# Packed attention and a split-precision MLP on one core: two sweeps over halves of w2's rows, with the attention placed between the products

## The chip, the core and the metric

The kernel runs on one core of a Trainium2 chip. Its time is the device time of one execution in microseconds (us). The runs of the kernel before were 879.05, 876.56 and 876.97 us, median 876.97. The engines are TensorE (PE, with its weight loads as PEld), VectorE (DVE), ScalarE (ACT), GpSimd (POOL) and SyncE (SP), whose queue issues every transfer of this kernel.

## The reference

For 8 batches and 8 heads, 32 packed queries `p` attend over the 576 tokens of `k` and `v`, then the 576 tokens of `q` attend over the 32 packed results. The output, laid out as 576 x 512 per batch, is mixed over the tokens with rank 32, and goes through a two-layer MLP with a residual.

```
p_packed = softmax(p k^T / 8) v          # (8, 8, 32, 64)
x        = softmax(q p_packed^T / 8) p_packed   # as (8, 576, 512)
u        = x + (x^T U V)^T
out      = u + relu(u w1) w2             # w1 512 x 2048, w2 2048 x 512
```

`U`, `V`, `w1` and `w2` arrive in 64-bit floating point and are turned into float32 on the chip.

## The kernel before, in words

**The algebra.** The second attention's weights times the packed values are never multiplied out. Per batch the kernel keeps A', the attention weights (8 heads x 32 packed tokens = 256 rows, as two groups `g` of 128 partitions, by 576 tokens) with the token mixing added. u is A' times a block matrix of the packed values, so u w1 is A' times W' (256 x 2048), where W' is the packed values times w1, one *fold* per pair of heads. The MLP of one batch is then, for each of 16 blocks `kt` of 128 hidden columns, `gemm1(kt)` (A' with a piece of W' into PSUM `h_ps`, ReLU) and, one step later, `gemm2(kt-1)` (the ReLU's result with 128 rows of w2, summed over all kt in four PSUM tiles `o` of 128 tokens each). The last 64 tokens of two batches share one further product, `joint`, every second batch. `add_u` adds u itself (`residual`).

**The precision.** Every operand of these products is split into a high and a low part in fp32r, and `mm3` (L74) makes three products: high-high, high-low and low-high (lines 76 to 78 of the profile). ScalarE copies the high part, VectorE or GpSimd subtracts to get the low one. The first attention's score and value products take plain float32 operands (L325, L361, L362).

**The stages.** Stage A goes over 16 units, half a batch each: `k` is turned by VectorE's 32 x 32 transposes (`transposed`, L101), the scores of four heads come from one product with a block-diagonal `bdp` (L325), then come softmax, PE transposes (`a_turn`), the product with `v` (`a_pack`), and the folds of batches 0 to 3 (`fold`, through PSUM and `conv`/`fold` tiles to DRAM, `wsr`). Between them `some_w1` converts w1 (`float32_of`, L67 to L71: one ScalarE and four VectorE operations per 128 x 512 block, and a `split`, L122 to L124). The first batch's second attention (`attention(0)`) runs there too. The tile framework orders stage A; after `manual_schedule` (L534) everything stays in the order in which the code is written.

**The loop.** Over 8 batches of 16 kt each: `gemm1`, `gemm2`, loads and splits of W' pieces (`load_wt`, `split_wt`, L455 and L456), w2's conversion during batch 0, one of 16 steps of the attention of the next batch (`steps`), and the folds of batches 4 to 7 (`later`, with w1 loaded and converted a second time, stored in `wsc`). In the attention `q` is turned by VectorE, split, and multiplied in three fp32r products by a block-diagonal of the packed values (`scores`, L186). `store` copies the sums out through ScalarE and VectorE.

Of the kernel before, what the change touches and what calls it, by code (L numbers as in the profile page):

```python
# [15 lines left out]
DRAM = bass.MemoryType.DRAM  # L16


@with_exitstack
def packed_attention_mixer_kernel(  # L20
# [22 lines left out]

    nc = tc.nc
# [5 lines left out]
    P = 128  # L50
    NB = S // 32
    SM = 512
    NK = DF // P
    NU = 2 * B
    QW = 256
    scale = 1.0 / float(D) ** 0.5
    HALF = ((0, 256), (256, 320))
# [4 lines left out]

    def float32_of(x, t, raw):


        low, high = raw[:, :, 0], raw[:, :, 1]
        nc.scalar.activation(t, high.bitcast(F32), AF.Abs)  # L67
        nc.vector.tensor_single_scalar(t, t, LEAST, op=ALU.max)  # L68
        nc.vector.tensor_scalar(x, t.bitcast(I32), 3, 0x3FFFFFF8, op0=ALU.logical_shift_left, op1=ALU.bitwise_and)  # L69
        nc.vector.scalar_tensor_tensor(x, high, -0x40000000, x, op0=ALU.bitwise_and, op1=ALU.bitwise_or)  # L70
        nc.vector.scalar_tensor_tensor(x, low, 29, x, op0=ALU.logical_shift_right, op1=ALU.bitwise_or)  # L71
        return x.bitcast(F32)
# [10 lines left out]
    psT = ctx.enter_context(tc.tile_pool(name="psT", bufs=2, space=PSUM))  # L83

# [3 lines left out]
    bdq = const.tile([P, 4, P], F32, name="bdq")  # L88
    nc.gpsimd.memset(bdq, 0.0)

    wsr = [dram.tile([2 * H * NP, DF], F32, name=f"wsr{r}", tag=f"wsr{r}") for r in range(2)]
    wsc = {b: dram.tile([H * NP, DF], F32, name=f"wsc{b}", tag=f"wsc{b}") for b in range(B // 2, B)}


    def load_nat(pool, bufs, src, b, g):
        nat = pool.tile([P, NB * D], F32, name="nat", bufs=bufs)
        nc.sync.dma_start(out=nat, in_=src[b, 4 * g:4 * g + 4].rearrange("h (i c) d -> (h i) (c d)", c=NB))
        return nat

    def transposed(t, nat):  # L100
        nc.vector.transpose(  # L101
            t.rearrange("p h (i c) -> p c h i", c=NB),
            nat.rearrange("p (c h l) -> p c h l", h=2, l=32),
        )
        return t


    def weight_tiles(name):
        return [
            tuple(pipe.tile([P, DF], F32R, name=f"{name}{x}{i}", tag=f"w{x}{i}") for x in "hl") for i in range(4)  # L110
        ]

    def conv_tile(dtype):
        return pipe.tile([P, DM], dtype, name="os", bufs=3)

# [672 lines left out]
```

## Time and profile before

| | us |
|---|---|
| median of the three timed runs | 876.97 |
| profiled execution, its own time | 877.77 |
| its span, first to last instruction | 876.0 |
| PE busy | 827.1 (94%) |
| DVE busy | 518.6 (59%) |
| ACT busy | 374.6 (43%) |
| POOL busy | 258.6 (30%) |
| DMA queue, bytes and share of 16 engines | 97.75 MB, 35.9% |

The profiled execution took 0.8 us more than the median of the runs, and 1.8 us of it lie outside the span. Matmuls are pipelined: the next starts before the one ahead has ended, so the profile's mean of one matmul is its length and not what it adds to the engine's time. What it adds is read from the distance of two starts in the timeline. A float32 product leaves two matmul records, an fp32r product one.

### The profile page before, as it was taken

Reading aid. Unit: us, or ns where it says so; the run is one execution under the profiler, and the core shown is the slowest. Engines: PE = TensorE matmul, PEld = TensorE weight load, DVE = VectorE, ACT = ScalarE, POOL = GpSimd, SP = SyncE. Lnnn points to the kernel's source line nnn. Section 1 sums busy time; section 2 is a strip of 40 time slices with the busy share of each in tenths; the row PEclk is TensorE's granted clock in tenths of the full one; section 3 lists DMA queues with packets and bytes.
Section 4 is the critical chain, followed back from the end, with each engine's and each line's share of the span. In section 5 each row is a group of like instructions: output and inputs, shape, how many; then the busy total and the mean of one; then the engine's idle time right before and its main releaser. Section 6 shows DMA issues by size and latency. Waiting matters only on the chain.

```text
span 876.0 us, 12670 instructions
## 1 busy us (share of the span) xinstructions
PE 827.1 (94%) x4480; PEld 708.5 (81%) x4480; DVE 518.6 (59%) x1042; ACT 374.6 (43%) x960; POOL 258.6 (30%) x230
## 2 busy tenths in 40 slices
PE   4779898889999999999999999999999999999997
PEld 2556576677879888888888888988888889889886
DVE  7999986789767875577675443443543524432220
ACT  2557676534444554456554332233332322333220
POOL 3302353545443213132323232323241313221110
PEclk9989999999999999999999999999999999999999
DMA  9769775823333444344453103010301120002001
GB/s 316 237 208 331 213 225 207 256 87 126 128 100 108 120 148 124 97 121 121 124 172 85 52 19 112 26 56 13 112 25 64 62 62 25 25 13 96 25 1 60
DMA packets 59998, 98.55 MB, mean 112 GB/s; under 512 B 12192, under 2 KB 36768, under 8 KB 59936
## 3 DMA queue, kind: packets, MB, share of 16 engines
q1 hardware_dynamic: 59936, 97.75, 35.9%
q8 instruction: 35, 0.57, 0.3%
q14 instruction: 27, 0.22, 0.1%
HBM read 71.52 MB, written 26.21 MB: 112 GB/s over the span
## 4 chain that ended last, share of the span: by engine, by line
PE 72%; DVE 18%; DMA 4%; issue 3%; ACT 3%; SPq 0%; DVEq 0%; ACTq 0%
PE o L78 15%; PE o L76 14%; PE o L77 14%; PE h_ps L76 7%; PE h_ps L77 7%; PE h_ps L78 7%; DVE kT L101 4%; DVE os L70 2%; DVE os L69 2%; DVE os L71 2%; PE w_ps L595 2%; DVE natT L101 2%; DVE os L68 2%; DMA bits<-in_moe_w_ch_dram 1%; PE t_ps L228 1%
## 5 line engine op out<-in xcount | busy, mean ns | idle before, releaser
L643 DVE SCALAR_TENSOR_TENSOR hl<-h_ps,hh 128x256 fp32r<-128x256 f32 x256 | 104.1, 418 | 180.2 <-ACT hh L641 145.0
L78 PE MATMUL o<-w2h,hl 128*128 128x512 f32 x512 | 201.8, 394 | 0.0
L76 PE MATMUL o<-w2h,hh 128*128 128x512 f32 x512 | 200.9, 392 | 0.0
L77 PE MATMUL o<-w2l,hh 128*128 128x512 f32 x512 | 200.4, 391 | 0.0
L641 ACT ACTIVATE hh<-h_ps 128x256 fp32r<-128x256 f32 x256 | 96.1, 383 | 235.0 <-PE h_ps L78 232.0
L76 PE MATMUL h_ps<-ah,fold 128*128 128x256 f32 x496 | 149.7, 302 | 7.5 <-DVE hl L643 7.1
L456 POOL TENSOR_TENSOR fold<-fold 128x512 fp32r<-128x512 f32 x62 | 81.4, 1313 | 230.7 <-ACT fold L455 225.3
L77 PE MATMUL h_ps<-al,fold 128*128 128x256 f32 x496 | 146.5, 295 | 0.0
L78 PE MATMUL h_ps<-ah,fold 128*128 128x256 f32 x496 | 146.0, 294 | 0.0
L78 PEld LDWEIGHTS o<-w2h,hl 128*128 128x128 f32 x512 | 96.1, 188 | 21.3
L77 PEld LDWEIGHTS o<-w2l,hh 128*128 128x128 f32 x512 | 96.4, 188 | 17.6
L76 PEld LDWEIGHTS o<-w2h,hh 128*128 128x128 f32 x512 | 96.3, 188 | 16.7
L76 PEld LDWEIGHTS h_ps<-ah,fold 128*128 128x128 f32 x496 | 93.7, 189 | 14.7 <-DVE hl L643 11.5
L77 PEld LDWEIGHTS h_ps<-al,fold 128*128 128x128 f32 x496 | 93.9, 189 | 2.1
L78 PEld LDWEIGHTS h_ps<-ah,fold 128*128 128x128 f32 x496 | 93.8, 189 | 0.0
L184 POOL TENSOR_TENSOR nlo<-natT,nhi 128x576 fp32r<-128x576 f32 x32 | 46.0, 1453 | 114.8 <-ACT nhi L183 114.8
L68 DVE TENSOR_SCALAR os<-os 128x512 f32<-128x512 f32 (+2 forms) x51 | 39.5, 775 | 35.4 <-ACT os L67 35.4
L325 PE MATMUL s_ps<-kT,bdp 128*128 128x288 f32 x128 | 39.7, 460 | 9.5 <-DVE bdp L316 9.3
L183 ACT CAST nhi<-natT 128x576 fp32r<-128x576 f32 x32 | 20.7, 675 | 56.3 <-DVE natT L101 53.2
L101 DVE STREAM_TRANSPOSE kT<-nat 128x1152 f32<-128x1152 f32 x16 | 37.3, 2330 | 5.8 <-DMA nat<-in_k_dram 5.7
L325 PEld LDWEIGHTS s_ps<-kT,bdp 128*128 128x128 f32 x128 | 26.4, 215 | 17.6 <-issue 9.3
L124 POOL TENSOR_TENSOR w1l<-os,w1h 128x512 fp32r<-128x512 f32 x16 | 21.2, 1328 | 62.3 <-ACT w1h L123 62.3
(145 smaller groups left out, 1419.7 us busy)
## 6 DMA issues: line engine op xcount, KB each, us to landing
bits<-in_moe_w_ch_dram SPq DMA_DIRECT2D x48, 512.0 KB, 4.3
nat<-in_k_dram SPq DMA_DIRECT2D x16, 576.0 KB, 4.9
nat<-in_q_dram SPq DMA_DIRECT2D x16, 576.0 KB, 4.5
vt<-in_v_dram SPq DMA_DIRECT2D x16, 512.0 KB, 5.5
wsr<-fold SPq DMA_DIRECT2D x32, 256.0 KB, 3.7
out_dram<-bits SPq DMA_DIRECT2D x16, 512.0 KB, 3.0
wsc<-bits SPq DMA_DIRECT2D x64, 128.0 KB, 2.2
fold<-wsc SPq DMA_DIRECT2D x32, 256.0 KB, 2.8
```

Source lines behind the costliest of these rows:

```text
L68: nc.vector.tensor_single_scalar(t, t, LEAST, op=ALU.max)
L76: nc.tensor.matmul(ps, lhsT=lh, rhs=rh, start=start, stop=False)
L77: nc.tensor.matmul(ps, lhsT=lh, rhs=rl, start=False, stop=False)
L78: nc.tensor.matmul(ps, lhsT=ll, rhs=rh, start=False, stop=stop)
L101: nc.vector.transpose(t.rearrange("p h (i c) -> p c h i", c=NB), nat.rearrange("p (c h l) -> p c h l", h=2, l=32),)
L124: nc.gpsimd.tensor_tensor(lo, x, hi.bitcast(F32), op=ALU.subtract)
L183: nc.scalar.copy(hi[:, dh], t)
L184: nc.gpsimd.tensor_tensor(lo[:, dh], t, hi[:, dh].bitcast(F32), op=ALU.subtract)
L325: nc.tensor.matmul(s_ps[:, hf, :288], lhsT=bdp[b % 2][:, 2 * g + dh], rhs=kT[:, dh, 288 * hf:288 * hf + 288], start=dh == 0, stop=dh == 1)
L456: nc.gpsimd.tensor_tensor(lo, raw, hi.bitcast(F32), op=ALU.subtract)
L641: nc.scalar.activation(hi, src, AF.Relu)
L643: nc.vector.scalar_tensor_tensor(lo, src, 0.0, hi.bitcast(F32), op0=ALU.max, op1=ALU.subtract)
```

## The change

**Two sweeps.** The loop goes over all 8 batches twice, `sw` 0 with rows 0 to 1023 of w2 (8 kt, `NKS`) and `sw` 1 with the others. Sweep 0 stores the sums of each batch in DRAM (`sums`, `sumj`), sweep 1 loads them (`load_sums`) and adds them on VectorE as it stores the output. A' goes to DRAM after each attention (`asp`) and is loaded again for sweep 1 (`reload_a`). w2's second half is converted during sweep 0, stored split (`w2d`) and loaded between the sweeps (`reload_w2`). w1 is converted once, half of its columns ahead of or at the start of sweep 0, half later; all folds are done by `fold`, four times four per batch pair `r`.

**What runs ahead of the loop.** Only the first attention of batches 0 and 1 (`packs`), the second attention of batch 0, five conversions and four folds. Everything else, `packs` of batches 2 to 7, `attention` of 1 to 7, 27 conversions and 60 folds, stands between the loop's products. The class `Chains` decides where, as the program is built: each chain is a generator that yields an assumed PE cost, a wait and a due time; `side.place(dt)` after every half `gemm1` and every quarter `gemm2` lets the ready chain with the earliest due time take one step; `side.until(name)` places steps until a chain is done, with no product between.

**The attention.** `k` and `q` are turned by PE transposes in pairs of tokens (`turn`, L302) and copied from PSUM by ScalarE and VectorE. The scores take eight float32 products per group, one for each head `h` and parity `r` of the token, 64 rows of `xT` by 32 columns (`scores`, L321), each in a place of its own of the PE array. The product with `v` takes 20 float32 products of 32 columns and 64 values each (L393). Block-diagonals and the split of `q` are gone.

```diff
+    def until(self, name):
+        while not (name in self.done and self.done[name] <= self.now or name in self.flags):
+            if not self.place():
+                self.now += 0.25
...
+    def turn(x, t):
+        pairs = x.rearrange("p a x -> p (a x)")
+        for h2 in range(2):
+            t_ps = bank()
+            for a in range(4):
+                c = 4 * h2 + a
+                nc.tensor.transpose(t_ps[:, P * a:P * a + P], pairs[:, P * c:P * c + P], ident)
+            nc.scalar.copy(t[:, 2 * h2:2 * h2 + 2, HT:HS], t_ps.rearrange("p (h x) -> p h x", h=2))
+            yield 0.45, 0.0
...
+    def scores(lT, t, g):
+        ss = [bank() for _ in range(2)]
+        for h in range(4):
+            hs = slice(32 * h, 32 * h + 32)
+            for r in range(2):
+                rs = slice(64 * r, 64 * r + 64)
+                nc.tensor.matmul(ss[r][hs, :HS], lhsT=lT[rs, g, hs], rhs=t[rs, h, HT * (1 - r):HT * (1 - r) + HS], start=True, stop=True)
+        return ss
...
+            for kk in range(5):
+                rows = P if kk < 4 else 64
+                for h in range(4):
+                    hs = slice(32 * h, 32 * h + 32)
+                    rhs = vk[:, kk, h] if kk < 4 else vx[:rows, 4, D * h:D * h + D]
+                    nc.tensor.matmul(p_ps[hs, :D], lhsT=eT[:rows, kk, hs], rhs=rhs, start=kk == 0, stop=kk == 4)
...
+        for c in cs:
+            for pr in range(4):
+                w_ps = bank()
+                mm3(w_ps, (lwh[:, pr], lwl[:, pr]), w1_slices(pr, c), True, True)
+                st = out_tile()
+                nc.scalar.copy(st, w_ps)
+                nc.sync.dma_start(out=wsr[r, c][P * pr:P * pr + P], in_=st)
+                yield 0.7, 0.0
...
+    together(packs(0))
+    uv = load_uv()
+    together(packs(1))
+    prepare_uv(*uv)
...
+    together(attention(0), in_turn(convert(first, converted), fold(0, (0,))))
...
+                if (sw, b) == (0, 0) and j == 2:
+                    side.until("w1_3_1")
+                    side.until("fold0_1")
...
+                if sw == 0 and b % 2 == 1 and j == 4 and b + 1 < B:
+                    side.until(f"fold{(b + 1) // 2}")
```

Three places of the instruction order show it. The first is PE at the first attention of a unit of stage A, before. `s_ps` are the scores, `kT` the turned keys, `bdp` the block-diagonal queries, `e` the exponentials and `pp_ps` the packed values.

```order
L325 MATMUL s_ps<-kT,bdp_97 128x288 x4
L345 MATMUL t_ps<-ident,e_146 128x128 x4
L346 MATMUL t_ps<-ident,e_146 64x128
L325 MATMUL s_ps<-kT,bdp_97 128x288 x4
L361 MATMUL pp_ps<-vt,eT 128x256 x4
L362 MATMUL pp_ps<-vt,eT 128x256
```

The same engine at a unit of the changed kernel, ahead of its loop (`xt` is a loaded tile, `xT` the turned one, `t_ps` every PSUM tile):

```order
L309 MATMUL t_ps<-ident,xt 128x128 x8
L315 MATMUL t_ps<-ident,xt 128x32 x4
L328 MATMUL t_ps<-xT,pT 32x288 x8
L338 MATMUL t_ps<-ident,e_241 128x128 x4
L340 MATMUL t_ps<-ident,e_241 64x128
L393 MATMUL t_ps<-xt,eT 32x64 x20
L399 MATMUL t_ps<-ident,two 128x128
```

Four products of 128 columns became eight of 32 columns, five of 128 became twenty of 32, and twelve transposes stand ahead. In the order before, the next unit's scores stand ahead of this unit's product with `v`; now one unit stands whole behind the other.

The second place is PE in batch 0 of the changed loop, from the last quarter of `gemm2(0)` to `gemm1(2)`; `w1h` and `w1l` are the split columns 512 to 1023 of w1.

```order
L121 MATMUL o<-w2h_754,hl 128x512
L353 MATMUL t_ps<-ident,pn 128x128 x2
L309 MATMUL t_ps<-ident,xt 128x128 x8
L315 MATMUL t_ps<-ident,xt 128x32 x4
L309 MATMUL t_ps<-ident,xt 128x128 x8
L315 MATMUL t_ps<-ident,xt 128x32 x4
L328 MATMUL t_ps<-xT,pT 32x288 x8
L328 MATMUL t_ps<-xT,ppT 32x288 x8
```

Before, six products of the next batch's scores are all that stands between `gemm2(0)` and `gemm1(2)`:

```order
L78 MATMUL o<-w2h_1446,hl 128x512
L76 MATMUL s_ps<-nhi,bqh 128x288
L77 MATMUL s_ps<-nlo,bqh 128x288
L78 MATMUL s_ps<-nhi,bql 128x288
L76 MATMUL s_ps<-nhi,bqh 128x288
L77 MATMUL s_ps<-nlo,bqh 128x288
L78 MATMUL s_ps<-nhi,bql 128x288
L76 MATMUL h_ps_1650<-ah,wt_1461 128x256
```

The rows of the changed order go on with a third unit of scores, the product with `v` and the twelve products of `fold0_1`, and only then comes `gemm1(2)`.

The third place is DVE, behind the evacuation of `gemm1(1)` in the changed loop (`hjl` is the low part for the joint product; L178 to L184 are the four conversion operations):

```order
L591 SCALAR_TENSOR_TENSOR hjl<-h_ps_924,hjh 128x32
L178 TENSOR_SCALAR ts<-ts 128x512
L179 TENSOR_SCALAR wd<-ts 128x512
L183 SCALAR_TENSOR_TENSOR wd<-bits,wd 128x512
L184 SCALAR_TENSOR_TENSOR wd<-bits,wd 128x512
L178 TENSOR_SCALAR ts<-ts 128x512
L179 TENSOR_SCALAR wd<-ts 128x512
L183 SCALAR_TENSOR_TENSOR wd<-bits,wd 128x512
L184 SCALAR_TENSOR_TENSOR wd<-bits,wd 128x512
L317 COPY xT<-t_ps 64x4x32
```

Before, the same place behind `gemm1(1)` read:

```order
L643 SCALAR_TENSOR_TENSOR hjl<-h_ps_1591,hjh 128x64
L68 TENSOR_SCALAR os<-os 128x512
L69 TENSOR_SCALAR os<-os 128x512
L70 SCALAR_TENSOR_TENSOR os<-bits,os 128x512
L71 SCALAR_TENSOR_TENSOR os<-bits,os 128x512
L196 STREAM_TRANSPOSE e<-s_ps 128x288
```

So one conversion stood between the evacuations of two kt; now seven conversions stand between those of `gemm1(1)` and `gemm1(2)`, with the attention's operations among them.

1015 lines of the change are left out of this document (481 added, 534 removed).

## The prediction

> **What bounds the kernel now.** I read the page first: the busy shares, then the slices.
>
> ```profile
> span 876.0 us, 12670 instructions
> PE 827.1 (94%) x4480; PEld 708.5 (81%) x4480; DVE 518.6 (59%) x1042; ACT 374.6 (43%) x960; POOL 258.6 (30%) x230
> ...
> PE   4779898889999999999999999999999999999997
> ...
> DVE  7999986789767875577675443443543524432220
> ```
>
> PE is full from about the ninth slice; VectorE is nearly full in the first seven. Busy times by stretch give the border (the first column is the stretch, then us, PE, PEld, DVE, ACT, POOL, clock, DMA share, GB/s):
>
> ```profile
> 0.00:50.00 50.00, 29.89 (x116) 21.04 (x116) 43.27 (x76) 22.26 (x57) 15.58 (x26) 0.97 0.86 277
> 100.00:150.00 50.00, 43.03 (x189) 31.54 (x188) 40.84 (x73) 35.43 (x83) 21.83 (x17) 0.94 0.69 219
> 300.00:400.00 100.00, 99.79 (x561) 87.37 (x560) 65.95 (x129) 49.55 (x117) 25.29 (x21) 1.00 0.41 121
> ```
>
> In stage A VectorE and the transfers are near their limit and PE waits; from 300 us PE has no gap. The timeline of PE tells where the loop begins, what one step costs, and where it ends.
>
> ```profile
> 160.18 0.39 PE L78 MATMUL w_ps<-w1h,lwl 128*128 128x512 f32 x1
> 160.41 0.28 PE L76 MATMUL h_ps<-ah,wt 128*128 128x256 f32 x1
> ...
> 699.69 0.40 PE L76 MATMUL o<-w2h,hjh 128*128 128x512 f32 x1
> ...
> 708.79 0.28 PE L76 MATMUL h_ps<-ah,fold 128*128 128x256 f32 x1
> ...
> 713.13 0.28 PE L76 MATMUL h_ps<-ah,fold 128*128 128x256 f32 x1
> ...
> 717.47 0.29 PE L76 MATMUL s_ps<-nhi,bqh 128*128 128x288 f32 x1
> ...
> 718.26 0.28 PE L76 MATMUL h_ps<-ah,fold 128*128 128x256 f32 x1
> ...
> 859.41 0.28 PE L76 MATMUL o<-rdh,ajh 128*128 128x256 f32 x1
> 859.53 0.28 PE L77 MATMUL o<-rdl,ajh 128*128 128x256 f32 x1
> ...
> 871.12 0.39 PE L78 MATMUL o<-w2h,hjl 128*128 128x512 f32 x1
> 871.55 0.58 ACT L684 COPY os<-o 128x512 f32<-128x512 f32 x1 [12.72 <-PE o L78]
> ```
>
> The loop runs from 160.4 to about 871.4, 711 us. One kt takes 713.13 - 708.79 = 4.34 us; a product of 512 columns in the joint (708.79 - 699.69) / 39 = 0.233; of 288 columns (718.26 - 717.47) / 6 = 0.13; of 256, 0.12. So 128 kt are 555.5, 192 joint products 44.8, 240 residual products 28.8: 629 us in both kernels. Before, seven attentions (24 products of 288, 10 transposes, 15 products of 256, 4 of 288: 6.6 us each, 46), 64 later products of 512 (15) and 16 transposes (2) stand beside it: 692, and 19 us of the loop are waits, half of them one wait, in the list of waits (total, times, longest):
>
> ```profile
> PE h_ps L76 <- DVE hl L643: 9.7, 8, 2.2
> ```
>
> **The change, part by part.** *Gained:* stage A's 160 us ahead of the loop, of which a shorter prologue stays. *Added:* its work inside a loop in which PE is already the bound. So the question is what that work takes on PE, and the price of one piece is not in this trace: a float32 product in a part of the array. What the trace shows is the whole-array form.
>
> ```profile
> 82.69 0.65 PE L325 MATMUL s_ps<-kT,bdp 128*128 128x288 f32 x2
> 83.18 0.63 PE L345 MATMUL t_ps<-ident,e 128*128 128x128 f32 x4
> 83.78 0.27 PE L346 MATMUL t_ps<-ident,e 128*64 128x128 f32 x1
> ```
>
> One float32 product of 288 columns leaves two records and holds PE for 83.18 - 82.69 = 0.49 us, 0.245 a record; four transposes take 0.60, at most 0.15 each (I take 0.12, as for the 256-column products). Eight such scores cost between 0.5 us, all places streaming at once, and 8 x 0.49 = 3.9, one after the other. Twenty products of 64 columns, by columns 64/288 of 0.49 = 0.109 each, cost between 0.55 (four places at once) and 2.2.
>
> I take a value between. A product's second record uses the same place as its first and must follow it; if records start in program order, the next place's first record can only run beside the second one of the place ahead. Eight scores then take nine records, 2.2 us, and the twenty products 21 halves of 0.109, 1.15 us. The Trainium skill, "TensorE: Matmul & The Clock Gate", section "Part 3: Packing small matmuls", says that matmuls stay in strict order and that places overlap with starts about 4 ns apart; by the second half of that, eight scores would take about 0.5 us and the sum would come out as in the first rival. No run here shows either yet.
>
> The loop then has, beside the 629: 208 transposes of the loaded tiles, 130 backwards and 24 small ones at 0.12 (43), 104 transposes of 32 rows (0.06 assumed, 6), 70 and 28 mixing products (12), 180 fold products of 0.233 (42): 103. With 26 groups of scores at 2.2 (57) and 12 of twenty products at 1.15 (14) the loop is 629 + 103 + 71 = 803 us.
>
> *The other engines in the loop.* The rows of VectorE, GpSimd and ScalarE that move or set the prologue (behind the bar: busy us, mean ns):
>
> ```profile
> L68 DVE TENSOR_SCALAR os<-os 128x512 f32<-128x512 f32 x48 | 38.2, 796 | 35.4 <-ACT os L67 35.4
> L69 DVE TENSOR_SCALAR os<-os 128x512 int32<-128x512 int32 x48 | 31.6, 658 | 1.8
> L70 DVE SCALAR_TENSOR_TENSOR os<-bits,os 128x512 int32<-128x512 int32 x48 | 37.4, 779 | 1.3
> L71 DVE SCALAR_TENSOR_TENSOR os<-bits,os 128x512 int32<-128x512 int32 x48 | 35.6, 741 | 1.3
> L101 DVE STREAM_TRANSPOSE kT<-nat 128x1152 f32<-128x1152 f32 x16 | 37.3, 2330 | 5.8 <-DMA nat<-in_k_dram 5.7
> L124 POOL TENSOR_TENSOR w1l<-os,w1h 128x512 fp32r<-128x512 f32 x16 | 21.2, 1328 | 62.3 <-ACT w1h L123 62.3
> L201 DVE TENSOR_REDUCE m<-e 128x18 f32<-128x576 f32 x16 | 12.0, 749 | 0.3
> L202 POOL TENSOR_TENSOR e<-e,m 128x576 f32<-128x576 f32 x16 | 18.8, 1172 | 54.3 <-DVE m L201 47.4 <-DVE hl L643 6.9
> L214 POOL TENSOR_TENSOR e<-e,s 128x576 f32<-128x576 f32 x16 | 20.0, 1248 | 15.6 <-DVE s L210 10.8 <-ACT w1p L586 3.5 <-DVE sm L352 1.3
> L216 DVE STREAM_TRANSPOSE aT<-e 128x576 f32<-128x576 f32 x16 | 12.3, 771 | 10.9 <-POOL e L214 10.9
> L335 ACT ACTIVATE e<-s_ps,mx 128x576 f32<-128x576 f32 x16 | 11.8, 739 | 7.5 <-DVE mx L333 7.4
> L348 ACT COPY eT<-t_ps 128x512 f32<-128x512 f32 x16 | 9.3, 582 | 1.9 <-PE t_ps L345 1.8
> L455 ACT CAST fold<-fold 128x512 fp32r<-128x512 f32 x62 | 38.8, 625 | 0.2
> L456 POOL TENSOR_TENSOR fold<-fold 128x512 fp32r<-128x512 f32 x62 | 81.4, 1313 | 230.7 <-ACT fold L455 225.3 <-issue 4.9
> ```
>
> A conversion is 2.97 us of VectorE. The 2.33 us transposes (32, 75 us) go; PSUM copies take their place. Outside batch 0 a batch of sweep 0 gives VectorE 27 to 41 us and ScalarE 28 to 39 us of work by such rows, against 50 us or more of PE: hidden, as is the second small ReLU piece per kt. In sweep 1 VectorE has about 15 us in 37 to 45, so that its adding of the stored sums costs nothing. A', sums and w2 in DRAM add some 46 MB to the 97.75 MB that took 35.9% of the engines' time: hidden as long as SP issues in time; if it doesn't, waits of the next kind grow.
>
> *Waits that the order makes.* (1) Batch 0: `fold0_1` stands in PE's order ahead of `gemm1(2)` and needs five conversions that begin behind `gemm1(1)`'s evacuation, 3.5 us in. VectorE has 5 x 2.97 = 15 us of them and some 5 us of attention between, then come ScalarE's copy and GpSimd's 1.33: 26 us. Until then PE has about 20 us to do: 6 us lost. VectorE's own wait for PE is in that. (2) Batch 1, kt 4: `until("fold1")` puts the end of the unit and 24 fold products in one row. Eight results go out through three `ev` tiles, each held for a 0.59 us copy and a store. The page's list of transfers has (issue to landing):
>
> ```profile
> wsr<-fold SPq DMA_DIRECT2D x32, 256.0 KB, 3.7
> fold<-wsc SPq DMA_DIRECT2D x32, 256.0 KB, 2.8
> ```
>
> That is 4.3 / 3 = 1.4 us a fold and not 0.7: 6 us, and 3 for the chain through the scaled values ahead of it. (3) Batch 4's `until("attention4")`: 4 us. (4) Seven other edges at 0.7: 5. Together 24 us; none to 45 are the bounds.
>
> *The prologue.* Nothing covers it: one unit stands whole behind the other. Loads land at about 6.5 us (the first `k` tile of before landed at 5.7). A unit is turning with two 0.58 copies 1.9, scores 2.2, two half reductions and a minimum 0.9, two half exponentials 1.1, transposes and a copy 1.3, products 1.15, scaling, transpose and copy 0.9, nine handoffs: 10.8. A handoff of 0.15 is an estimate; the last product above ends at 871.51 and its copy begins 0.04 later, the least it can be. Four units and 3 us for the conversions between them: 53. Then two groups of turning and scores (8.2), the softmax by the rows of L201, L202, L335, L214 and L216, its sum at the price of its maximum and two 0.5 us transposes at half of a 576-column one's (6.4 with small ones, and 1.4 of handoffs), the transposes back, the mixing and the last fold (4.3), its copy, store, load, split and issues (0.6 + 3.7 + 2.8 + 0.6 + 1.3 + 0.8 = 9.8). The loop begins at 83 us, 160 before.
>
> *The sum*, made against the profiled execution of 877.8 (876.0 and 1.8 around it; the median is 0.8 lower): 83 + 803 + 24 + 5 (from the last product to the end, 876.0 - 871.4 before) + 1.8 = 917 us. The prologue gives back 77 us, the loop takes 111 more of PE and 5 more of waits. 917 is the number for the median too.
>
> **Rivals.** *All places at once.* The 26 groups of scores cost 0.55 and the products 0.6: 21 in place of 71, so the loop is 753. In the prologue 6 groups save 1.65 and 4 products 0.55: 71. Waits rise to 30, since PE has less to do in batch 0. 71 + 753 + 30 + 7 = 861 us, faster than before. It decides as soon as eight scores take under about 0.9 us. For it: the change's own `yield 0.55` assumes it; against it: two records per float32 product, back to back in the trace.
>
> *No overlap.* 26 x 3.9 + 12 x 2.2 = 128: loop 860, prologue 83 + 6 x 1.7 + 4 x 1.05 = 97, waits 20: 984 us. For it: no two matmuls of the trace overlap in their streaming.
>
> *The waits are covered.* In any of these the 24 us could be near none, since the chains' own waits were set to be covered; this moves each case down by 20 at most and changes the sign of none.
>
> **How the numbers follow.** Forecast (pairs overlap) 0.43, all at once 0.41, no overlap 0.16. The forecast's own range is 895 to 950, the first rival's 845 to 880. The range 845 to 950 leaves out the third case. A measurement here tells 0.3% (2.6 us) from no change. Faster: 0.41 x 0.87 and 0.43 x 0.05, 0.38; same 0.04; slower 0.58.
>
> **What would show it.** Right: eight L328 products with 0.2 to 0.3 us between the starts of places, some 2.2 us a group; the first `h_ps` at 75 to 90 us; a gap on PE ahead of `gemm1(2)` and a slow row of folds in batch 1; from batch 9 on PE without gaps at 4.34 us a kt. Wrong: groups of scores under 1 us (the time falls below 877) or near 3.9; a loop that begins after 95 us; waits on VectorE or on loads in sweep 1, which this sum has at none.

## The result, and the profile after

The changed kernel takes 1005.62 us (median of four runs, 1001.01 to 1006.33) against 876.98 of the kernel before in the same rounds: 1.146 times as long, with an interval of 1.142 to 1.150. It is slower, as forecast, but by 129 us where the forecast said 40, and outside the range of 845 to 950. One execution of the kernel of experiment 13 took 1647.14 us where its others took 976 to 981; nothing on record says why, and it is in no figure below.

The page of the changed kernel, the rows that answer to those shown of before (busy shares, then the slices):

```profile
span 999.2 us, 15578 instructions
PE 867.1 (87%) x5536; PEld 708.3 (71%) x5536; DVE 411.3 (41%) x1140; ACT 364.9 (37%) x1057; POOL 196.6 (20%) x193
...
PE   4564579879899697998997799969999999999998
...
DVE  4542776253365445352466832212322322323232
...
PEclk9986679889999898999998999979999999999999
```

PE does 40 us more and its share falls from 94 to 87%. Its row has holes up to the 27th slice, and the row of the granted clock has dips at nearly the same places. VectorE is never near its limit. The same in stretches, cut where batches begin (batch 0; 1 to 3; 4 to 6; 7; 8; 9 to the end of the loop); the clock stands after the five engines:

```profile
92.70:177.40 84.70, 65.69 (x429) 50.02 (x430) 55.90 (x118) 37.77 (x97) 29.51 (x26) 0.80 0.37 112
177.40:398.80 221.40, 190.65 (x1408) 145.54 (x1406) 103.20 (x276) 94.95 (x261) 50.69 (x51) 0.93 0.51 163
398.80:592.30 193.50, 171.66 (x1139) 136.19 (x1136) 96.43 (x244) 82.03 (x226) 51.02 (x48) 0.96 0.42 131
592.30:627.60 35.30, 35.30 (x197) 31.22 (x196) 9.64 (x34) 11.94 (x40) 8.04 (x12) 1.00 0.38 123
627.60:698.80 71.20, 60.63 (x302) 50.97 (x300) 14.30 (x52) 26.53 (x74) 5.15 (x4) 0.93 0.58 198
698.80:994.00 295.20, 295.20 (x1680) 262.79 (x1679) 89.77 (x301) 77.79 (x284) 34.79 (x27) 1.00 0.35 113
```

From 698.8 us on, and in batch 7, PE has no gap and the full clock. What went wrong in the loop lies in the other stretches: batches 0 to 6, which hold the attentions and conversions, and batch 8. The timeline of PE (and one row of VectorE) gives the loop's begin, one kt of sweep 1, and the end:

```profile
92.70 0.61 PE L119 MATMUL h_ps<-ah,wth 128*128 128x288 f32 x1 [11.15 <-ACT wth L520]
...
739.05 0.29 PE L119 MATMUL h_ps<-ah,wth 128*128 128x288 f32 x1
...
743.38 0.39 PE L119 MATMUL o<-w2h,hjh 128*128 128x512 f32 x1
...
994.14 0.39 PE L121 MATMUL o<-w2h,hjl 128*128 128x512 f32 x1
994.57 0.69 DVE L667 TENSOR_TENSOR ev<-o,partj 128x512 f32<-128x512 f32 x1 [5.35 <-PE o L121]
```

A kt takes 743.38 - 739.05 = 4.33 us there, as forecast. The waits of PE, by who ended them (total, times, longest):

```profile
PE t_ps L119 <- ACT lwh L493: 14.7, 4, 8.8
PE t_ps L338 <- ACT e L371: 13.0, 5, 4.2
PE h_ps L119 <- ACT wth L520: 11.1, 1, 11.1
PE t_ps L338 <- DVE aT L434: 9.4, 8, 3.5
PE t_ps L328 <- DVE xT L317: 8.3, 7, 2.9
PE t_ps L315 <- ACT xT L310: 8.1, 7, 3.1
PE o L119 <- ACT ev L615: 7.0, 1, 7.0
PE o L119 <- DVE ev L613: 6.5, 2, 3.3
```

They belong to many chains, and few are long. The list covers the whole execution: 11.2 of the 13.0 us at L338 behind L371, 4.4 of the 9.4 behind L434 and 3.6 of the 8.3 at L328 lie ahead of the loop, and the 11.1 us at L520 end with the loop's first product. What each term of the forecast came to, in the profiled execution of 1001.0 us (PE's issue is the distance from one start to the next, without the idle time, summed over the trace; each distance is put down to the full or the halved clock by the granted clock of its moment):

| term, us | forecast | measured |
|---|---|---|
| prologue | 83 | 92.7 |
| main products (`h_ps`, `o`, joint, residual), at full clock | 629 | 651 |
| transposes, mixing, folds, at full clock | 103 | 108 |
| scores and products with `v` in places, at full clock | 71 | 31 |
| what PE loses at the halved clock | not in the sum | 30 |
| waits in the loop | 24 | 81.5 |
| from the last product to the end of the execution | 6.8 | 6.7 |
| sum | 917 | 1001 |

The halved clock's 30 us are those of the loop: PE worked 65 us of it at 0.50, and each form takes about twice as long there (a main product of 288 columns 262 ns in place of 137, of 512 columns 456 in place of 239). By batch the waits are 18.9, 11.2, 4.2, 15.3, 3.1, 5.6 and 12.7 us in batches 0 to 6, none in 7, 10.6 in 8, none after. A batch is counted from its first `h_ps` to that of the next.

**The scores.** A group of eight scores at full clock, with the two products that follow it at once (timeline of PE):

```profile
474.37 0.72 PE L328 MATMUL t_ps<-xT,pT 64*32 64x288 f32 x16
475.02 0.50 PE L119 MATMUL o<-w2h,hh 128*128 128x512 f32 x1
475.35 0.39 PE L120 MATMUL o<-w2l,hh 128*128 128x512 f32 x1
```

It costs 475.02 - 474.37 = 0.65 us. In the trace's records the first products of the eight places start at 474.371 to 474.418, 7 ns apart, and the second ones at 474.638 to 474.685: all places stream at once, first all first passes, then all second passes. That is the first rival's mechanism; the forecast's step of pairs fell. The Trainium skill, "TensorE: Matmul & The Clock Gate", "Part 3: Packing small matmuls", gives about 4 ns between the starts of places that overlap; the trace agrees on the overlap and has 7.

**How a wait comes about.** ScalarE in batch 0, as it stands in its order:

```profile
117.81 0.68 ACT L422 ACTIVATE e<-e 128x576 f32<-128x576 f32 x1 [3.94 <-POOL e L421]
118.40 1.05 ACT L310 COPY xT<-t_ps 128x512 f32<-128x512 f32 x2
```

and PE:

```profile
119.02 0.63 PE L315 MATMUL t_ps<-ident,xt 32*128 32x32 f32 x4 [2.70 <-ACT xT L310]
```

ScalarE stands 3.94 us at an exponential of the first group of `attention(1)`, for GpSimd's result. Behind it in its order stands the copy of the second group's turned `q`, which frees a PSUM tile, and PE has come to the transpose that needs the tile. Meanwhile VectorE and GpSimd work, one after the other, at what the exponential needs:

```profile
115.42 0.74 DVE L420 TENSOR_REDUCE m<-e 128x18 f32<-128x576 f32 x1
...
116.31 1.47 POOL L421 TENSOR_TENSOR e<-e,m 128x576 f32<-128x576 f32 x1 [1.67 <-DVE m L420]
```

The transposes that ScalarE is to copy need nothing of this; they end at 116.33, two us before the copy begins. So a copy waits for a step that it doesn't need, because ScalarE's order is fixed, and PE waits for the copy. The 7.0 us wait is of this kind as well (ScalarE's copy of `o`, L615, stands behind two conversion operations, of which one waits 2.41 us for VectorE and the other 1.17 for its load), and so are the two at L613 (VectorE waits for the store of an `ev` tile). The 8.8 us wait of batch 8 is a load that was issued late; ScalarE and SyncE's queue:

```profile
665.20 1.26 ACT L493 CAST lwh<-ppT 64x128 fp32r<-64x128 f32 x4 [4.58 <-DMA ppT<-ppTd]
```

```profile
652.45 0.32 SPq L243 DMA_DIRECT2D w2l<-w2d15l  x1
653.21 1.23 SPq L515 DMA_DIRECT2D raw<-wsr  x2
...
658.62 0.79 SPq L485 DMA_DIRECT2D ppT<-ppTd  x2
```

The fold's packed values are asked for at 658.6, behind the loads of w2's second half.

### The profile page after: what moved, and what is told of

It is laid out like the page before. It is cut to its first block, busy times and chain, and to the rows that moved or that the text cites. A ratio compares the mean times of both kernels' runs of the same rounds, so it can differ in the third digit from the quotient of the medians.

```text
span 999.2 us, 15578 instructions
## 1 busy us (share of the span) xinstructions
PE 867.1 (87%) x5536; PEld 708.3 (71%) x5536; DVE 411.3 (41%) x1140; ACT 364.9 (37%) x1057; POOL 196.6 (20%) x193
## 5 line engine op out<-in xcount | busy, mean ns | idle before, releaser
L521 POOL TENSOR_TENSOR wtl<-raw,wth 128x512 fp32r<-128x512 f32 x64 | 83.4, 1304 | 442.5 <-ACT wth L520 417.8
L119 PE MATMUL h_ps<-ah,wth 128*128 128x288 f32 x512 | 158.1, 309 | 11.5 <-ACT wth L520 11.1
L121 PE MATMUL h_ps<-ah,wtl 128*128 128x288 f32 x512 | 153.3, 299 | 0.5 <-POOL wtl L521 0.5
L120 PE MATMUL h_ps<-al,wth 128*128 128x288 f32 x512 | 153.1, 299 | 0.0
L119 PEld LDWEIGHTS h_ps<-ah,wth 128*128 128x128 f32 x512 | 98.6, 192 | 21.5 <-ACT wth L520 11.4
L120 PEld LDWEIGHTS h_ps<-al,wth 128*128 128x128 f32 x512 | 98.7, 193 | 3.8
L121 PEld LDWEIGHTS h_ps<-ah,wtl 128*128 128x128 f32 x512 | 98.3, 192 | 0.8 <-POOL wtl L521 0.8
L309 PE MATMUL t_ps<-ident,xt 128*128 128x128 f32 x256 | 45.2, 315 | 11.1 <-ACT ppT L400 2.6
L310 ACT COPY xT<-t_ps 128x512 f32<-128x512 f32 x64 | 36.8, 586 | 35.6 <-PE t_ps L309 35.5
L589 ACT ACTIVATE hjh<-h_ps 128x32 fp32r<-128x32 f32 x256 | 49.6, 194 | 0.0
L520 ACT CAST wth<-raw 128x512 fp32r<-128x512 f32 x64 | 39.6, 621 | 19.3 <-DMA raw<-wsr 19.1
L591 DVE SCALAR_TENSOR_TENSOR hjl<-h_ps,hjh 128x32 fp32r<-128x32 f32 x256 | 46.2, 180 | 0.0
```

Source lines behind the costliest of these rows:

```text
L119: nc.tensor.matmul(ps, lhsT=lh, rhs=rh, start=start, stop=False)
L120: nc.tensor.matmul(ps, lhsT=lh, rhs=rl, start=False, stop=False)
L121: nc.tensor.matmul(ps, lhsT=ll, rhs=rh, start=False, stop=stop)
L309: nc.tensor.transpose(t_ps[:, P * a:P * a + P], pairs[:, P * c:P * c + P], ident)
L310: nc.scalar.copy(t[:, 2 * h2:2 * h2 + 2, HT:HS], t_ps.rearrange("p (h x) -> p h x", h=2))
L520: nc.scalar.copy(hi, raw)
```

## The experiments

Six theories were tested. A: TensorE waits at steps of the side chains whose data isn't there yet (each expectation says which steps). B: the conversions hold the chains up, with the folds and stores in experiment 10. C: waits halve the clock, which makes them dearer. D and E: the tiles for results, or SyncE's order, are what the queues stand at. F: batch 0 waits for its fold. The changed kernel's own runs spread over 5 us (8 with a fifth one of 1008.80), so that smaller effects are read from the traces. There a single batch varies too: batch 3, in which experiment 7 changes no instruction, takes 78.4 us there and 75.8 in the changed kernel, so that less than 3 us in one batch says nothing. Each time is given with what it stands against; where nothing is said that is the profiled 1001.0.

**1 and 2. All planned waits of the chains doubled, and halved.**

```diff
-            c[1] = self.now + wait
+            c[1] = self.now + 2.0 * wait
```

> Every wait that a chain asks for before its next step is doubled as the program is built; the work is the same. Theory A, the steps stand too early for the engines that feed them: PE's idle time in the loop falls from 81 us to under 50, the half clock with it, and the time to 950 to 975 us. Rival, there are too few places, and what is put off comes together where the program places steps until a chain is done: fewer waits inside the batches, longer ones ahead of kt 4 of batches 1, 3 and 5, and 990 to 1030 us.

Measured: 1019.5 us (one run). Theory A's gain did not come; its rival holds in the main. Steps that are held back come together where the order waits for a chain: batch 1 takes 102.6 us in place of 83.4, batch 5 78.0 in place of 62.0. Batches 2, 4 and 6 shrink by 5 to 8 us, and batch 3, which the rival named too, stays as it was.

```diff
-            c[1] = self.now + wait
+            c[1] = self.now + 0.5 * wait
```

> All planned waits of the chains are halved, where the first experiment doubled them. Theory A (the planned waits are too short, so TensorE stands at steps whose data isn't there): waits grow by 20 us or more, 1020 to 1050 us. Rival (the waits come from bursts, since steps that are held back are placed together where the order waits for a chain): steps are spread more evenly, 980 to 995 us.

Measured: 1050.54 us (1048.59 to 1052.49), 1.198 (1.191 to 1.205) times before. Theory A holds on this side: the waits in the loop rise from 81.5 to 114 us. Of the three factors tried, a half, one and two, one is the best: with shorter planned waits steps come before their data, with longer ones they come in bursts.

**3. VectorE's four conversion operations left out in the loop.** ScalarE writes in their place; the values are not converted.

```diff
-            float32_1(xi, t, mine)
+            if loop["on"]:
+                nc.scalar.activation(xi.bitcast(F32), mine[:, :, 1].bitcast(F32), AF.Abs)
+            else:
+                float32_1(xi, t, mine)
...
-            x = float32_2(xi, mine)
+            x = xi.bitcast(F32) if loop["on"] else float32_2(xi, mine)
```

> The 27 conversions of the loop keep their load, one ScalarE operation, the split and the stores, but leave out VectorE's four operations, 80 us of it, so that w1 and w2 are wrong there. Theory B, the conversions fill VectorE's queue ahead of what PE waits for: batches 0, 2, 3 and 6, which hold them, lose 40 us and the time falls to 955 to 970. Theory A, the latency of the attention's own steps is what PE waits for: batch 0 gains 10 us, the others next to nothing, and the time stays at 985 to 995.

Measured: 976.3 us (one run), between the two theories. Batch 0 shrinks from 84.7 to 69.8 us, batch 6 from 68.6 to 62.6, batches 1 to 4 change by under 1. So the conversions make some 25 us, 15 of them in batch 0. VectorE is busy for 56 of 84.7 us there, so it isn't full; that the operations cost by where they stand in its order, and not by their length, is likely but not shown, since the edit takes away both.

**4. Every group of scores twice**, the second time into the same tiles.

```diff
+        for h in range(4):
...
+                nc.tensor.matmul(ss[r][hs, :HS], lhsT=lT[rs, g, hs], rhs=t[rs, h, HT * (1 - r):HT * (1 - r) + HS], start=True, stop=True)
```

> Each group of eight scores is made twice into the same place, 32 groups more, 26 of them in the loop. If all places run at once, as the starts in the trace say (two passes of 0.24 us), 0.5 us a group and PE's busy time 13 us longer in the loop: 1010 to 1020 us in all. If pairs overlap, as the forecast had it, 2.2 us a group and 1055 to 1075.

Measured: 1017.1 us (one run), in the range of all places at once. The trace says it better, since the loop also begins 9.5 us later: at full clock a group made twice costs 1.13 us where one costs 0.65, so that the second pass of eight adds 0.49. All places at once holds.

**5. Waits of two lengths put into sweep 1**, where PE has none: a copy and 1 or 4 GpSimd operations between two products.

```diff
+    def gap(n):
...
+        nc.scalar.copy(st, t_ps)
+        for _ in range(n):
+            nc.gpsimd.tensor_tensor(st, st.bitcast(F32), st.bitcast(F32), op=ALU.subtract)
+        nc.tensor.matmul(bank(), lhsT=vs[:, :P], rhs=st, start=True, stop=True)
...
+                if sw == 1 and 2 <= b <= 6 and j == 3:
+                    gap(1 if b % 2 == 0 else 4)
```

> In sweep 1, which has no waits, PE is made to wait ahead of the fourth kt of batches 2 to 6: a product, a ScalarE copy, one GpSimd operation (batches 2, 4, 6; about 2.5 us) or four (batches 3 and 5; about 6.5 us), and a product that needs them. Theory C, a wait also lowers the granted clock: the long ones are followed by stretches at half clock, each 3.4 us or more, and the five cost over 28 us for 21 us of waits, 1029 us or more. Rival, the clock falls by what the side steps do and not by waiting: no half clock in sweep 1, about 1022.

Measured: 1023.2 us (one run). That is near the rival's time, because the waits came out at 1.8 and 5.1 us and not at 2.5 and 6.5; what decides is the clock. The busy times around a short and a long wait (clock after the five engines):

```profile
758.80:760.60 1.80, 0.02 (x1) 0.00 (x0) 0.00 (x0) 0.59 (x1) 1.04 (x1) 1.00 1.04 312
760.60:764.00 3.40, 3.39 (x20) 3.10 (x21) 1.05 (x4) 0.95 (x4) 0.00 (x0) 1.00 1.06 319
...
798.80:800.80 2.00, 0.04 (x1) 0.00 (x0) 0.00 (x0) 0.59 (x1) 1.18 (x2) 1.00 1.08 300
800.80:804.00 3.20, 0.02 (x1) 0.02 (x1) 0.00 (x0) 0.00 (x0) 2.97 (x3) 0.50 0.97 317
804.00:807.60 3.60, 3.60 (x14) 3.50 (x15) 0.52 (x2) 0.47 (x2) 0.00 (x0) 0.50 0.01 4
807.60:811.00 3.40, 3.40 (x20) 2.91 (x18) 0.52 (x2) 0.47 (x2) 0.00 (x0) 0.99 0.02 5
```

All three waits of 1.8 us leave the clock at 1.00. Both of 5.1 us halve it 2.0 us after they begin, and it comes back 3.6 us after PE resumed, having issued 14 products where 20 are usual. The batch with a wait of 1.8 us takes 2.5 more, with the two added products in it; that with 5.1 takes 7.5 more: beyond the wait and these two (0.7) 1.7 us, half of the 3.6. Theory C holds: each of these two long waits cost itself and about 1.7 us.

**6. The same shown the other way: PE kept busy in its waits** with products that nobody reads.

> Adds 96 products that nobody reads, 22 us of TensorE, in the three longest waits of the loop: 40 ahead of the loop's first product (wait 11.1 us), 24 ahead of the joint product between batches 5 and 6 (7.0), 32 ahead of the fold of the last batch of sweep 0 (8.8). Theory C (the clock halves because TensorE waits): the halved stretches of 84.9 to 98.6, 532.1 to 538.9 and 661.8 to 672.0 us go, the main products behind these waits start at full clock, and the kernel is faster by half of the 14.5 us that TensorE works in them: 7 us, 992 to 996 against 1001. Rival (the clock falls for another reason, such as the transfers or the work before): the stretches stay and the time is 1000 to 1006.

Measured: 1011.54 us (1009.54 to 1013.55), 1.154 (1.147 to 1.161). The rival's sign, but the experiment missed its mark: the 40 products ran at 23.9 us, far ahead of the wait, and the 32 went to the fold of batch 7, whose wait was none. Only the 24 ahead of the joint product stood in theirs; 1.8 of 7.0 us were left, and the clock halved all the same, for 3.4 us in place of 6.8. For the waits that were meant nothing follows. (What the 40 products did where they ran is told in the last section.) So it was done again:

```diff
+                if (sw, b, j) == (0, 0, 0):
+                    fill(76, cur.al[:, 0])
                 cur.gemm1(kt)
...
+        if (r, cs[0]) == (2, 2):
+            fill(62, w1_slices(0, 2)[0])
```

> As the run before with filled waits, with the products nobody reads now where the waits are: 76 of 256 columns right ahead of the loop's first product, 62 ahead of the first product of the fold that waits 8.8 us in the first batch of sweep 1. Theory C (the clock halves because TensorE waits): the halved stretches of 84.9 to 98.6 and 661.8 to 672.0 us go or shorten to their parts that lie in what is left of the waits, products behind them start 0.12 (256 columns) and 0.23 us (512) apart, and the stretch from the first batch of sweep 1 to the next, 71.2 us, takes 68 to 69. Rival: the halved stretches stay and the batch takes 71 or more.

Measured: 1007.5 us (1006.03 to 1008.98), 1.148 (1.143 to 1.154), no difference in the whole. At the two places it did what theory C says. PE at the fold of batch 8:

```profile
665.35 7.59 PE L478 MATMUL t_ps<-w1h 128*128 128x256 f32 x62
...
673.95 0.50 PE L119 MATMUL t_ps<-w1h,lwh 128*128 128x512 f32 x1 [1.01 <-ACT lwh L498]
674.77 0.40 PE L119 MATMUL o<-w2h,hh 128*128 128x512 f32 x1
```

In the changed kernel the fold's first product and the next `o` start 667.95 - 666.51 = 1.44 us apart:

```profile
666.51 0.80 PE L119 MATMUL t_ps<-w1h,lwh 128*128 128x512 f32 x1 [8.78 <-ACT lwh L493]
667.95 0.63 PE L119 MATMUL o<-w2h,hh 128*128 128x512 f32 x1
```

With the filling it is 0.82, the clock stays at 1.00 from 650 to 683 us, and the batch takes 68.3 us in place of 71.2, with 7.6 us more work on PE. The halved stretch at the loop's begin shrinks from 13.7 us to 3.4, and yet batch 0 isn't shorter (86.0 us against 84.7): only 5.9 of the 13.7 us lay behind the loop's first product, and by later stretches batch 0 has as much halved clock as before, 34 us against 33. Batch 5 takes 65.8 us against 62.0, though nothing was put into it; why, no run shows.

**7. A longer planned wait behind the reload of the packed values.**

```diff
-                yield 0.0, 4.0
+                yield 0.0, 14.0
```

> The plan gives 14 in place of 4 between the loads of the stored packed values and the fold that reads them. Theory A (each wait of TensorE is a chain whose planned wait was too short, and the halved clock of 661.8 to 672.0 us is that wait's own): the 8.8 us wait ahead of the fold of the last batch of sweep 0 and the 2.7 us that the halved clock behind it costs both go, 1001 - 11.5, 987 to 993 us. Rival (the fold stands at its due time anyway and the products behind it wait for it): the wait comes back at the next place where the order waits for a fold, 997 us or more.

Measured: 995.28 us (994.98 to 995.58), 1.135 (1.131 to 1.140). The expectation names the wrong batch: the 8.8 us wait is that of the first batch of sweep 1, batch 8. It and the halved stretch behind it are gone; batches 7 to 9 take 139.4 us in place of 146.8. Theory A holds for this wait, with 7.4 us of the 11.5; the time lies between the two ranges.

**8. Four tiles for results.**

```diff
-        return pipe.tile([P, 512], I32, name="wd", bufs=2)
+        return pipe.tile([P, 512], I32, name="wd", bufs=1)
...
-        return pipe.tile([P, 512], dtype, name="ev", bufs=3)
+        return pipe.tile([P, 512], dtype, name="ev", bufs=4)
```

> Four tiles in place of three for the results that leave through stores (ev), paid for with one in place of two tiles in the conversions. Theory D (the three tiles are what the evacuations wait for): the waits of TensorE that end with a copy into such a tile, 3.3 at 191.8, 3.2 at 335.9 and 7.0 at 535.2 us and the small ones among the folds, go down by two thirds, and the halved clock behind them: 985 to 993 us. Rival (the copies stand behind other work in VectorE's and ScalarE's order, whatever the number of tiles): 998 to 1008.

Measured: 984.16 us (983.61 to 984.70), 1.122 (1.118 to 1.125). Of the two waits for VectorE's copy (L613), 6.5 us, one of 0.7 is left, and batches 1 and 2 take 77.1 and 58.1 us in place of 83.4 and 62.3. The 7.0 us wait is still 6.7. Theory D holds for VectorE's copies and not for ScalarE's, which stands behind conversion operations. The loop also begins 4.1 us earlier. Why, the runs don't say: it begins as early in experiment 10, where TensorE, ScalarE and VectorE have the same order as in the changed kernel up to there.

**9. Stores issued by ScalarE.**

```diff
-                nc.sync.dma_start(out=wsr[r, c][P * pr:P * pr + P], in_=st)
+                nc.scalar.dma_start(out=wsr[r, c][P * pr:P * pr + P], in_=st)
```

(the same for ScalarE's half of `sums`, and for `sumj`)

> The stores of folds, and of those sums that ScalarE copies, are issued by ScalarE right behind its copy, so that SyncE no longer stands at them with the loads behind it. Theory E (loads come late because SyncE waits for copies ahead of them in its order): the waits that end at a load or behind one (8.8 us at 666.5, 7.0 at 535.2, 2.3 at 466.7) shrink to under half, 983 to 993 us. Rival (loads are late because they are issued late or tiles are short): 998 us or more; ScalarE pays some 0.1 us for each of 80 issues.

Measured: 1011.58 us (1008.44 to 1014.72), 1.153 (1.144 to 1.162). Theory E falls for this way of doing it. The waits of 7.0 and 2.3 us are still 7.0 and 2.7. The one of 8.8 is gone, but in the same batch one of 7.0 stands at a copy into an `ev` tile (L662). And the edit has a price that the expectation had too low: each of the 84 stores takes ScalarE 0.33 us to issue, not 0.1.

**10. Both attentions of batches 2 to 7 left out** (they use the stored A' and packed values of batches 0 and 1).

```diff
-            side.add(f"packs{b}", line(0, b - 2, 1 if b % 2 else 5), packs(b),
...
-        side.add(f"attention{b}", line(0, b, 0) - 0.5, attention(b),
...
+            side.flags.update((f"packs{b}", f"attention{b}") if b > 1 else ())
+    side.add("attention1", line(0, 1, 0) - 0.5, attention(1))
```

> Leaves out both attentions of batches 2 to 7: those batches load the stored A' of batches 0 and 1, and their folds the packed values of these two, so that the loop keeps all main products, conversions, folds and stores, and one attention. Of TensorE's loop it takes 31 us of tiled products, 57 us of transposes and mixing. Theory A (most waits are the chains of the attention): waits and halved clock together fall from 111 us to 45 or less, 1001 - 88 - 66, 835 to 855 us. Rival B (conversions, folds and stores in the same queues make them): 70 us or more are left, 875 to 900 us.

Measured: 854.1 us (one run). The time is theory A's, and the reason is not. PE's issue fell by 106 us at full clock and not by 88: without side work between them main products of 512 columns stand 230 ns apart, with it 239 (252 in batches 0 to 6). Waits and halved clock fell from 111 us to about 76 (56.8, and half of 39), where A had 45 or less and B 70 or more. The rows of batch 0, and of batch 8:

```profile
88.60:174.20 85.60, 60.30 (x296) 47.19 (x297) 52.56 (x106) 36.08 (x87) 29.25 (x24) 0.76 0.38 123
...
480.90:551.90 71.00, 60.46 (x302) 50.79 (x301) 14.30 (x52) 26.53 (x74) 5.15 (x4) 0.93 0.58 198
```

Batch 8 is as it was, 71.0 us against 71.2. Batch 0 takes 85.6 us against 84.7, but it isn't the same batch: the plan moved other steps to where the attentions had stood. It makes 12 folds in place of 4, and the 16 conversions that the changed kernel has in batches 2, 3, 5 and 6 stand in batches 1 to 3. Batches 4 to 7 have no wait, and no side step is left in them. So the run shows that folds, conversions and one attention, packed into batches 0 to 3, still make 46 us of waits; it doesn't show what the attentions of later batches cost batch 0.

**11. Both attentions ahead of the loop again.**

```diff
+    for b in range(2, B):
+        together(attention(b - 1), packs(b))
+    together(attention(B - 1))
...
```

> Undoes one part of the change: both attentions of batches 2 to 7 and the second one of batch 1 stand ahead of the loop again, one unit of the first beside one of the second, and the loop loads A' from DRAM. Two sweeps, transposes by TensorE, scores and packed products in places stay. Theory A (the chains inside the loop cost more than they hide): the loop shrinks by 150 us or more to 750 and less, the prologue grows by 6 units of 20 to 25 us to some 220 us: 945 to 985 us, faster than the changed kernel. Rival (TensorE's work is the same wherever it stands, and the prologue has the same chains without cover): 1005 to 1050 us.

Measured: 1029.34 us (1028.94 to 1029.73), 1.173 (1.169 to 1.177). The loop shrinks by 154 us to 748, as theory A said; the prologue grows by 183:

```profile
275.63 0.29 PE L119 MATMUL h_ps<-ah,wth 128*128 128x288 f32 x1
```

where one wait comes back seventeen times:

```profile
PE t_ps L338 <- ACT e L371: 45.5, 17, 5.7
```

The rival's time holds. Placing this attention between the products is worth some 24 us against this way of doing it ahead.

**12. The two edits that helped, together:** the diffs of 7 and 8.

> The two edits that made the changed kernel faster alone, together: 14 planned between the loads of the stored packed values and their fold, and four tiles for results with one for conversions. If they act on different waits (the 8.8 us wait of the first batch of sweep 1, the copies into tiles of sweep 0): 984 - 8, 973 to 979 us. If they act on the same order of copies and stores: 981 to 986.

Measured: 973.96 us (971.12 to 975.95), 1.109 (1.106 to 1.113). They add up: 10 us of experiment 7 and 21 of experiment 8 against the median, 32 together. It is the best version tried of the changed kernel, and still 96 us behind the one before.

**13. With these two, the fold for which batch 0 waits made ahead of the loop.**

```diff
+    first += [(f"w1_{pr}_1", 0, parts_w1(pr, 1)) for pr in range(4)]
-    together(attention(0), in_turn(convert(first, converted), fold(0, (0,))))
+    together(attention(0), in_turn(convert(first, converted), fold(0, (0, 1))))
...
```

> As the run with both edits, and the conversion of w1's columns 512 to 1023 and their twelve fold products stand ahead of the loop, beside the second attention of batch 0. Theory F (batch 0 waits because the order waits for this fold): batch 0 shrinks from 86 us by 20 or more, and the prologue grows by less than 12, since VectorE has 12 us more there: 960 to 969 us. Rival (batch 0's waits are its attention chains, seven conversions of w2 and the early steps, whatever the fold): batch 0 shrinks by the fold's own PE time and a few us, the prologue grows as much: 974 us or more.

Measured: 977.07 us (median of three, 975.66 to 980.68), 1.114 (1.110 to 1.118), against 973.96. Theory F falls: batch 0 goes from 86.2 to 81.8 us, its waits from 19.7 to 16.4, and the loop begins 8.9 us later.

## Why the prediction was wrong

*What bounds the kernel.* Right: PE is the bound, a kt costs 4.33 us, and sweep 1 has no gap from batch 9 on. Also right is that the change adds more to PE's loop than the prologue gives back. By the table even a loop without a wait and at full clock would end at 92.7 + 790 + 6.7 = 889 us, behind the 877 of before.

*The tiled products.* "The next place's first record can only run beside the second one of the place ahead" fell. Eight scores take 0.65 us, not 2.2, and twenty products 0.83, not 1.15: 31 us in place of 71 in the loop, and some 11 less ahead of it. Taken alone this would have made the forecast 866, on the other side of the 877 of before. The first rival had the mechanism, and its 861 us were wrong all the same: of the 140 us that it lacks, 81 are waits and halved clock (111, where it had 30), 37 PE's work in the loop (790, where it had 753) and 22 the prologue (92.7, where it had 71).

*The failed step: "Together 24 us; none to 45 are the bounds".* Measured are 81.5 us, and 30 more by the halved clock that these waits bring with them, which is in no term of the sum, though the stretches of stage A that the prediction prints show a clock of 0.97 and 0.94. The places that the forecast names came out near its sum: (1) the row of side steps ahead of `gemm1(2)` in batch 0, 6 us, has 13.7; (2) that ahead of kt 4 of batch 1, 9 us, has 5.5; (3) that ahead of batch 4, 4 us, has 4.9. That is 24 in place of 19. What failed is (4), "Seven other edges at 0.7: 5": 57 us of waits lie elsewhere. The forecast looked for places where the order names a chain (`until`). 41 of the 57 us stand ahead of steps that the plan put between the products by itself, and 16 ahead of main products, most of them for a copy that frees a PSUM tile. In the waits followed up above the copy or load that PE needed stood behind other work in the order of ScalarE, VectorE or SyncE; how many of the 57 us are of that kind wasn't counted.

*"Hidden, as is the second small ReLU piece".* The sums of busy time are right: ScalarE and VectorE are at 37 and 41%. That is no argument for a loop in which each side step needs PE, a copy, and PE again, in orders fixed beforehand. Experiment 3 gave back 25 us (against the profiled execution) and experiment 8 21 us (against the median) on engines that were half idle.

*Main products, 651 and not 629.* The step "629 us in both kernels" fails by 22 us: beside side steps the products of 512 columns stand 252 ns apart in batches 0 to 6 at full clock, 229 in sweep 1. Before, the same products take about 635 us of the trace. So "19 us of the loop are waits" was a reading too high as well: PE's idle time in the loop of before is 10.6 us, and the 9.7 shown are eight waits, not one.

*The prologue*, 92.7 and not 83. PE's last products ahead of the loop end at 81.6 and not at 73 (83 - 9.8), and the wait for the first W' piece is 11.1 us and not 9.8. With the measured price of the tiled products the forecast's own sum would have been some 72, so that it is 20 us short. What it lacks is again the clock: PE ran at half of it until 64.4 us and from 67.8 to 78.1 (last section), 44 us of its work; half of that, 22 us, is an estimate of what this cost.

*"Waits on VectorE or loads in sweep 1, which this sum has at none".* 10.6 us in batch 8, 8.8 of them a load behind others in SyncE's queue (experiment 7).

Open: most of batch 0's excess. VectorE's conversions make 15 us of it (3). Its fold makes little (13), and experiment 10 can't say what the attentions of later batches do. By the list of waits of batch 0, 7.6 of its 18.9 us end with ScalarE's copies of turned tiles (L310) and 4.0 with exponentials (L371).

## What to carry to other kernels

Before moving work between the products of an engine that is already the bound, add up what it adds to that engine with no wait at all: here that sum alone, 889 us at the prices measured, already lost. Then count the handoffs and not the busy times: in fixed orders each step that goes to another engine and back can stand behind the wait of another, and half-idle engines prove nothing. Waits of several us on TensorE, and a prologue in which it works half of the time, are to be priced with the halved clock that goes with them.

## What the runs showed that was not expected

**When the clock halves.** The halved stretches are multiples of 3.41 us on a grid that goes through the whole run, and what goes with them is how much of one such step PE was busy. In the changed kernel a wait of 2.3 us inside one step of the grid, and the step after it:

```profile
463.80:467.20 3.40, 1.10 (x8) 0.69 (x7) 0.59 (x3) 0.42 (x3) 0.00 (x0) 1.00 1.10 307
467.20:470.60 3.40, 3.40 (x12) 2.61 (x12) 0.00 (x0) 1.17 (x2) 0.00 (x0) 0.50 0.05 12
```

and a longer one, 2.95 us, that lies across two steps:

```profile
556.00:559.40 3.40, 1.76 (x12) 1.28 (x10) 2.99 (x3) 1.60 (x5) 2.32 (x2) 1.00 0.00 0
559.40:562.80 3.40, 2.09 (x21) 1.30 (x22) 3.27 (x11) 0.99 (x3) 1.29 (x1) 1.00 0.02 5
562.80:566.20 3.40, 3.40 (x22) 3.07 (x21) 2.56 (x6) 1.44 (x6) 2.23 (x2) 1.00 0.00 0
```

1.10 us of PE in 3.4 halves the next step, 1.76 and 2.09 don't. In experiment 5 the same wait of batch 6 (2.92 us there) fell into one step of the grid, with PE busy for 1.09 us of it, and the clock halved behind it for 6.8 us. PE worked 6.2 us of them: the same wait cost about 3 us of PE's rate more, or nothing, by where it fell. Where exactly the border lies stays open. In all traces here every step at full clock with under 1.5 us of work was followed by half clock and none with over 2.6; between the two both were seen. The Trainium skill, "TensorE: Matmul & The Clock Gate", "Part 1: The HAM clock gate", has windows of 3413 ns that run freely, which these traces agree with, and the half rate after an idle window; here a window with a third of it busy was enough.

**The prologue ran at half clock.** The first slices of the row PEclk show 9, but the trace has no record of the clock before 64.43 us. The spacing of equal products tells it: eight transposes take 1.92 us in the prologue, as they do in batch 0 where 0.50 is on record, and 1.04 in the prologue of experiment 6's first kernel, where 1.00 is:

```profile
17.90 1.92 PE L309 MATMUL t_ps<-ident,xt 128*128 128x128 f32 x8
...
114.36 1.97 PE L309 MATMUL t_ps<-ident,xt 128*128 128x128 f32 x8 [0.61 <-DVE e L417]
```

```profile
38.77 1.04 PE L309 MATMUL t_ps<-ident,xt 128*128 128x128 f32 x8
```

The transposes of loaded tiles stand 213 ns apart up to 64 us, against 109 where the clock is at 1.00. PE works 36 us of these 64. In experiment 6 the 40 products at 23.9 us brought the full clock: it is at 1.00 from 27.7 to 41.4 us, and at 0.50 for 41 us behind that.

**Small steps between the products.** The next product behind a group of scores starts 0.33 us ahead of its follower (475.02 and 475.35 in the timeline) and not 0.23; 700 products of batches 0 to 6 at 252 ns and not 229 are 16 us.
